# One DMA per store, k and q as one tile, and a new order in a fused attention and MLP kernel

## Chip, cores, metric

The kernel runs on one core of one Trainium2 chip. The time is the device time of one execution in microseconds, and a quoted time is the median of several runs. Each experiment was timed next to the kernel before, in alternating rounds on the same chip. Chips differ a little: the kernel before took 361.2 to 364.1 us on the ones used here. So each experiment is judged by its ratio to the kernel before of its own call. Ratios use fast runs only; where a run was slow (over 1.5% above the fastest of the same kernel), the text says so.

## The reference

Eight batches, eight heads, 576 tokens and 64 channels per head. Attention with random features, then a token mix of rank 32, then a two-layer channel MLP with a residual. All inputs and the output are float32.

```python
def phi(x):                                       # 128 random features: cos and sin
    proj = np.einsum('bhsd,md->bhsm', x, omega)
    return np.concatenate([np.cos(proj), np.sin(proj)], axis=-1) / np.sqrt(m)
q_p, k_p = (phi(q), phi(k))
kv = np.einsum('bhsm,bhsd->bhmd', k_p, v)
z = np.sum(k_p, axis=2)
num = np.einsum('bhsm,bhmd->bhsd', q_p, kv)
den = np.einsum('bhsm,bhm->bhs', q_p, z)          # kept away from zero
x = (num / den)                                   # heads joined: 8 x 576 x 512
# ...
h = x.transpose(0, 2, 1) @ U @ V                  # token mix
u = x + h.transpose(0, 2, 1)
out = u + np.maximum(u @ w_ch1, 0.0) @ w_ch2      # 512 -> 2048 -> 512
```

## The kernel before

Two heads are a group and two groups are a quad. A quad's k, q and v are three loads. k and q of the first four quads are transposed on TensorE; those of the other twelve go through DMA transposes. ScalarE makes the sines and cosines. TensorE then makes `kv` (L416) and `num` (L430), VectorE divides, and a batch's x is complete. The token mix gives u; a DMA transpose on SyncE's queue gives `uT`; then follow the two layers, w1 (L585) and w2 (L605), the residual (L621) and the store (L628).

The program order of all engines is one long string of words. An instruction waits for its operands, but each engine, and each queue that issues DMAs, takes its work in that order.

```python
ORDER = """
begin first/k om ident gate first/q ld/k/0 warm ld/q/0 ldv/0 ld/k/1 cast/k/0 cast/k/1 ...
# ... about 1100 words: load, transpose, layer 1 of batch b, layer 2, store
"""
# ...
rawp = ctx.enter_context(tc.tile_pool(name="rawp", bufs=2))
outp = ctx.enter_context(tc.tile_pool(name="outp", bufs=3))
# ...
held["v", n] = rawp.tile([P, 2, NS * D], F32, name="vraw", bufs=1)       # v of a quad, 576 KB
(nc.sync if n else nc.gpsimd).dma_start(held["v", n], quad(v, n))
# ...
def tpd(name=name, n=n):                                                  # k and q apart
    nc.sync.dma_start_transpose(transposed(name, n), held.pop((name, n)).rearrange("p i e -> p (i e)"))
# ...
def ut0(p=p, cs=cs):                                                      # first token mix, transposed
    t_ps = one(("ut0", p))
    for t in range(NT):
        nc.tensor.matmul(t_ps[:, t * P:(t + 1) * P], held["x", 0][:, t, cs], ident, start=(t == 0), stop=False)
    nc.tensor.matmul(t_ps, held["hu", 0][:, cs], Vb[:, 0:SM], start=False, stop=True)
# ...
add(("tu", b), SP, lambda b=b: nc.sync.dma_start_transpose(
    new_uT(b).rearrange("p t c s -> p (t c) s"), held["u", b].rearrange("p t c -> p (t c)")), ...)
# ...
def store(b=b, t=t, cs=cs, es=(0, 1), by=nc.sync):
    for e in es:
        if b == TAIL:
            dst = out[2 * t + e].rearrange("(p s) c -> p s c", s=NS)[:, 8, cs]
        else:
            dst = out[b].rearrange("(p s) c -> p s c", s=NS)[:, 2 * t + e, cs]
        by.dma_start(dst, held["o", b, t][e * TL:(e + 1) * TL, cs])
```

Token `9*p + 2*t + e` of a batch lies in tile t on partition `64*e + p`, with p from 0 to 63. So one output tile (128 partitions x 512) is two sets of 64 tokens, e = 0 and e = 1. Each set is a regular pattern in memory: 64 rows of 2 KB, nine rows apart. Each store is one DMA per set. The ninth tokens of two batches share the tiles of a "tail" batch.

## Time and profile before

| | before |
|---|---|
| median of 3 runs | 364.13 us |
| span of the profiled run | 359.2 us |
| TensorE (PE) busy | 342.2 us, 95% |
| PE not busy, first 36 us | 36.00 − 25.82 = 10.2 us |
| PE not busy, all the rest | 17.0 − 10.2 = 6.8 us, 4.4 us of it after the last matmul |

From the profile page of the kernel before come the span, busy time of each engine, then rows with one digit per fortieth of the span (9 is 90% or more busy, `PEclk` is the granted TensorE clock in tenths), then the chain of work that ended last by engine, and two kinds of DMA issues with size and median time to landing.

```profile
span 359.2 us, 8233 instructions
PE 342.2 (95%) x3565; PEld 181.2 (50%) x3565; DVE 193.4 (54%) x284; ACT 216.4 (60%) x223; POOL 117.7 (33%) x103
...
PE   4769999999999899999999999999999999999995
...
PEclk9979999999999999999999999999999999999999
DMA  8999899699998895936679705504204145002133
...
PE 85%; DMA 8%; DVE 2%; POOL 2%; issue 1%; ACT 1%; POOLq 0%; DVEq 0%
...
out_dram<-o SPq DMA_DIRECT2D x70, 128.0 KB, 2.9
vraw<-in_v_dram SPq DMA_DIRECT2D x15, 576.0 KB, 4.8
```

TensorE bounds this kernel. After the third slice its row is nearly all nines, and it is 85% of the chain. The DMA engines are also near full for the first third. The loss that remains is in the opening, where the clock row has a 7.

From the wait lists of the kernel before: PE's three longest entries, then one of POOL's (engine, line, what it waited for: total us, times, longest).

```profile
PE ps L317 <- DVE kraw L286: 4.3, 1, 4.3
PE ps L317 <- DMA kraw<-in_k_dram: 3.2, 3, 1.6
PE ps L416 <- POOL vq L301: 1.7, 1, 1.7
...
POOL vq L301 <- DMA vraw<-in_v_dram: 16.7, 5, 6.9
```

All of PE's waits of more than half a microsecond but the 1.7 us are in the opening. Later there are none worth naming: every other transfer is there in time.

From the windows view of the kernel before (stretch, its length, then busy time of PE, PEld, DVE, ACT, POOL with counts, granted clock, DMA share, GB/s):

```profile
core 0: us, PE busy (x) PEld busy (x) DVE busy (x) ACT busy (x) POOL busy (x), PEclk, DMA share, GB/s
0.00:36.00 36.00, 25.82 (x422) 19.32 (x423) 28.18 (x51) 25.63 (x25) 27.14 (x36) 0.91 1.07 203
72.00:108.00 36.00, 35.76 (x480) 19.01 (x479) 26.98 (x38) 26.64 (x25) 15.68 (x14) 1.00 1.19 195
144.00:180.00 36.00, 36.00 (x468) 19.68 (x465) 25.39 (x37) 28.03 (x25) 12.99 (x9) 1.00 0.66 129
252.00:288.00 36.00, 36.00 (x375) 18.64 (x373) 11.05 (x23) 17.86 (x22) 5.51 (x4) 1.00 0.21 52
...
24.00:26.00 2.00, 1.87 (x46) 1.64 (x41) 1.94 (x3) 2.00 (x2) 1.88 (x6) 0.50 1.23 207
```

PE is all but gapless at full clock in the three later stretches, and at half clock from 22 to 28 us.

### The profile page before, as it was taken

Reading aid. Unit: us, or ns where it says so; the run is one execution under the profiler, and the core shown is the slowest. Engines: PE = TensorE matmul, PEld = TensorE weight load, DVE = VectorE, ACT = ScalarE, POOL = GpSimd, SP = SyncE. Lnnn points to the kernel's source line nnn. Section 1 sums busy time; section 2 is a strip of 40 time slices with the busy share of each in tenths; the row PEclk is TensorE's granted clock in tenths of the full one; section 3 lists DMA queues with packets and bytes.
Section 4 is the critical chain, followed back from the end, with each engine's and each line's share of the span. In section 5 each row is a group of like instructions: output and inputs, shape, how many; then the busy total and the mean of one; then the engine's idle time right before and its main releaser. Section 6 shows DMA issues by size and latency. Waiting matters only on the chain.

```text
span 359.2 us, 8233 instructions
## 1 busy us (share of the span) xinstructions
PE 342.2 (95%) x3565; PEld 181.2 (50%) x3565; DVE 193.4 (54%) x284; ACT 216.4 (60%) x223; POOL 117.7 (33%) x103
## 2 busy tenths in 40 slices
PE   4769999999999899999999999999999999999995
PEld 3557455454555464545555454554454544444443
DVE  3989858785888368758645654464132452001111
ACT  4796995749957777696946459536646303651200
POOL 6895670726434724146245124002302100000000
PEclk9979999999999999999999999999999999999999
DMA  8999899699998895936679705504204145002133
GB/s 207 223 234 150 150 190 162 145 187 203 208 186 185 187 215 111 227 53 100 139 195 202 149 2 114 144 2 86 63 2 124 31 93 113 0 2 58 29 70 79
DMA packets 68728, 45.09 MB, mean 126 GB/s; under 512 B 47444, under 2 KB 59860, under 8 KB 68692
## 3 DMA queue, kind: packets, MB, share of 16 engines
q1 hardware_dynamic: 55508, 29.98, 39.8%
q0 software_dynamic: 12816, 13.93, 24.2%
q8 instruction: 28, 0.46, 0.5%
q10 hardware_dynamic: 368, 0.66, 0.5%
q14 instruction: 8, 0.07, 0.1%
HBM read 37.18 MB, written 9.44 MB: 130 GB/s over the span
## 4 chain that ended last, share of the span: by engine, by line
PE 85%; DMA 8%; DVE 2%; POOL 2%; issue 1%; ACT 1%; POOLq 0%; DVEq 0%
PE ps L585 34%; PE ps L605 32%; PE ps L416 5%; PE ps L430 4%; DMA kraw<-in_k_dram 3%; DMA uT<-u 2%; DMA qraw<-in_q_dram 2%; PE ps L392 2%; PE ps L551 2%; PE ps L376 2%; DMA vraw<-in_v_dram 1%; DVE ang L353 1%; PE ps L493 1%; PE ps L435 1%; PE ps L317 1%
## 5 line engine op out<-in xcount | busy, mean ns | idle before, releaser
L402 ACT ACTIVATE ft<-ang 128x2304 bf16<-128x2304 int16 (+3 forms) x70 | 134.7, 1955 | 27.2 <-DVE ang L353 9.7
L598 ACT ACTIVATE hid<-ps 128x512 bf16<-128x512 f32 x144 | 82.5, 597 | 92.7 <-PE ps L585 92.4
L605 PE MATMUL ps<-W2b,hid 128*128 128x512 bf16 (+1 forms) x592 | 134.9, 374 | 0.0
L585 PE MATMUL ps<-uT,W1b 128*128 128x512 bf16 x512 | 119.9, 379 | 0.2 <-DMA uT<-u 0.2
L406 POOL TENSOR_SCALAR ang<-ang 128x2304 int32<-128x2304 int32 (+2 forms) x34 | 67.9, 2000 | 127.7 <-ACT ft L402 113.8
L353 DVE TENSOR_SCALAR ang<-ps 128x1280 int32<-128x1280 f32 (+2 forms) x66 | 85.1, 1317 | 34.7 <-PE ps L369 15.8
L605 PEld LDWEIGHTS <-hid 128*128 128x128 bf16 x592 | 55.5, 98 | 62.8 <-issue 2.3
L585 PEld LDWEIGHTS <-W1b 128*128 128x128 bf16 x576 | 53.9, 98 | 63.8 <-issue 1.4
L621 DVE TENSOR_TENSOR o<-ps,u 128x512 f32<-128x512 f32 x32 | 21.8, 686 | 65.2 <-PE ps L605 64.9
L301 POOL CAST vq<-vraw 128x1152 bf16<-128x1152 f32 x16 | 18.4, 1153 | 30.5 <-DMA vraw<-in_v_dram 16.7
L416 PE MATMUL ps<-vq,ft 64*128 64x65 bf16 x1152 | 25.9, 196 | 2.2 <-POOL vq L301 1.7
L416 PEld LDWEIGHTS <-ft 64*128 64x128 bf16 x1152 | 23.2, 97 | 9.2 <-issue 6.5
L446 DVE TENSOR_TENSOR x<-ps,rec 128x640 bf16<-128x640 f32 x32 | 26.4, 825 | 1.1
L430 PEld LDWEIGHTS <-ft 128*128 128x128 bf16 x512 | 20.2, 99 | 6.4 <-issue 0.8
L430 PE MATMUL ps<-kvb,ft 128*128 128x65 bf16 x512 | 21.6, 195 | 0.0
L420 DVE CAST kvb<-ps 128x260 bf16<-128x260 f32 x32 | 13.1, 423 | 15.3 <-PE ps L416 15.1
L553 DVE TENSOR_TENSOR u<-ps,x 128x1024 bf16<-128x1024 f32 x16 | 19.2, 1219 | 3.6 <-PE ps L551 3.5
L444 DVE RECIPROCAL ps<-ps 128x10 f32<-128x10 f32 x32 | 7.2, 225 | 19.0 <-PE ps L435 19.0
L585 PE MATMUL ps<-utailT,W1b 128*128 128x512 bf16 x64 | 14.6, 379 | 0.0
L392 PE MATMUL ps<-qT,WT 64*128 64x512 bf16 x64 | 14.0, 414 | 0.2 <-DVE ang L353 0.2
L376 PE MATMUL ps<-WT,kT 64*128 64x128 bf16 x256 | 13.8, 233 | 0.3 <-DVE qT L321 0.3
L376 PEld LDWEIGHTS <-kT 64*128 64x128 bf16 x256 | 9.4, 101 | 6.8 <-issue 5.7
(63 smaller groups left out, 152.5 us busy)
## 6 DMA issues: line engine op xcount, KB each, us to landing
out_dram<-o SPq DMA_DIRECT2D x70, 128.0 KB, 2.9
vraw<-in_v_dram SPq DMA_DIRECT2D x15, 576.0 KB, 4.8
kraw<-in_k_dram POOLq DMA_DIRECT2D x15, 288.0 KB, 6.7
qraw<-in_q_dram POOLq DMA_DIRECT2D x15, 288.0 KB, 7.4
W1b<-in_moe_w_ch_dram POOLq DMA_DIRECT2D x4, 512.0 KB, 10.1
W2b<-in_moe_w_ch_dram POOLq DMA_DIRECT2D x4, 512.0 KB, 9.5
vraw<-in_v_dram POOLq DMA_DIRECT2D x1, 576.0 KB, 5.3
ang<-in_k_dram ACTq DMA_DIRECT2D x1, 288.0 KB, 3.2
```

Source lines behind the costliest of these rows:

```text
L353: nc.vector.tensor_scalar(out=dst, in0=src, scalar1=TO_UNITS, scalar2=None, op0=ALU.mult)
L376: nc.tensor.matmul(pk[:, e, j * P:(j + 1) * P], kT[r, c, :], WT[r, :])
L392: nc.tensor.matmul(pq[:, e, :], WT[r, :], held["qT", n][r, c:c + 4, :])
L402: nc.scalar.activation(out=held["ft", g].rearrange("p f a c -> p f (a c)")[:, f, lo:hi], in_=low[:, lo:hi, 0], func=ACT.Sin, scale=TO_RAD)
L406: nc.gpsimd.tensor_scalar(out=ang, in0=ang, scalar1=TURN / 4.0, scalar2=1.0, op0=ALU.add, op1=ALU.mult)
L416: nc.tensor.matmul(kv_ps[:, hh, o], ft[r, f, 0, c:c + M], vq[n % NV][r, NS * (g % 2) + s, :], start=(s == 0), stop=(s == NS - 1))
L430: nc.tensor.matmul(nd[:, hh, t, :], ft[:, f, 1, c:c + P], kvb[:, hh, f, :], start=(f == 0), stop=(f == 1))
L446: nc.vector.tensor_tensor(out=x[:, :, hp * P:(hp + 1) * P].rearrange("p t (h d) -> p h t d", h=2), in0=nd[:, :, :, 0:D], in1=rec.unsqueeze ...
L585: nc.tensor.matmul(one(key), W1b[:, f // 4, ct, f % 4 * P:(f % 4 + 1) * P], uT[:, :, ct, :], start=(ct == 0), stop=(ct == NCT - 1))
L598: nc.scalar.activation(out=held["hid", b][:, f, :], in_=one(at_bank), func=ACT.Relu)
L605: nc.tensor.matmul(one(key)[:, 0:cs.stop - cs.start], held["hid", b][:, f, t * P:(t + 1) * P], W2b[:, f, cs], start=(f == 0), stop=(f == N ...
L621: nc.vector.tensor_tensor(out=held["o", b, t][:, cs], in0=one(key)[:, 0:cs.stop - cs.start], in1=u[:, t, cs], op=ALU.add)
```

## The change

The intent was to fill the opening and to issue fewer DMAs. It has five parts:

1. k and q of a quad share one raw tile and one transposed tile, and one DMA transpose moves both.
2. A store is one DMA of 256 KB, where it was two of 128 KB.
3. The first token mix is split in two: the product with x can start before the low-rank sum is ready, and its last copy is shared by VectorE and ScalarE.
4. Twenty matmuls on the identity matrix (128x512, results unused) stand in PE's order, most of them in the opening, to keep TensorE's clock up.
5. A new order of all the words.

```diff
-begin first/k om ident gate first/q ld/k/0 warm ld/q/0 ldv/0 ld/k/1 cast/k/0 cast/k/1 ld/q/1 omb tpp/k/0/0@2 ...
+begin first/k om ident first/q ld/k/0 d/0@6 warm d/1@2 ld/q/0 d/2@4 ld/k/1 d/3@0 d/4@5 ld/q/1 omb d/5@6 cast/k/0 ...
 (the rest of the order is cut)
+    for i in range(WARMERS):
+        def warmer(i=i):
+            nc.tensor.matmul(one(("d", i)), ident, ident.unsqueeze(1).to_broadcast([P, NT, P]))
 ...
-        if (name, n) not in held:
-            held[name, n] = rawp.tile([P, 2, NS * D], BF16, name=f"{name}raw")
-        return held[name, n]
+        if ("raw", n) not in held:
+            held["raw", n] = rawp.tile([P, 2, 2, NS * D], BF16, name="raw")
+        return held["raw", n][:, "kq".index(name), :, :]
 ...
-                def tpd(name=name, n=n):
-                    nc.sync.dma_start_transpose(transposed(name, n), held.pop((name, n)).rearrange("p i e -> p (i e)"))
-                add(("tp", name, n), SP, tpd, needs=[("ld", name, n)] + old)
+            def tpd(n=n):
+                transposed("k", n)
+                nc.sync.dma_start_transpose(held["T", n].rearrange("p j c s -> p (j c) s"), held.pop(("raw", n)).rearrange("p j i e -> p (j i e)"))
+            add(("tp", n), SP, tpd, needs=[("ld", "k", n), ("ld", "q", n)] + old)
 ...
-        def ut0(p=p, cs=cs):
+        def ut0x(p=p, cs=cs):
             (the four matmuls of x, on their own)
+        add(("ut0x", p), PE, ut0x, needs=[("x", p)], takes=1)
+        add(("ut0", p), PE, lambda p=p, cs=cs: nc.tensor.matmul(one(("ut0x", p)), held["hu", 0][:, cs], Vb[:, 0:SM], start=False, stop=True),
+            needs=[("huc0", p), ("ut0x", p)])
+        pieces = [(0, NT, SCA if p in (1, 2) else DVE)] if p < 3 else [(0, 2, DVE), (2, NT, SCA)]
 ...
-            def store(b=b, t=t, cs=cs, es=(0, 1), by=nc.sync):
-                for e in es:
-                    if b == TAIL:
-                        dst = out[2 * t + e].rearrange("(p s) c -> p s c", s=NS)[:, 8, cs]
-                    else:
-                        dst = out[b].rearrange("(p s) c -> p s c", s=NS)[:, 2 * t + e, cs]
-                    by.dma_start(dst, held["o", b, t][e * TL:(e + 1) * TL, cs])
+            def store(b=b, t=t, cs=cs, es=slice(0, 2), by=nc.sync):
+                if b == TAIL:
+                    dst = out[2 * t + es.start:2 * t + es.stop].rearrange("b (p s) c -> b p s c", s=NS)[:, :, 8, cs]
+                else:
+                    dst = out[b].rearrange("(p s) c -> s p c", s=NS)[2 * t + es.start:2 * t + es.stop, :, cs]
+                by.dma_start(dst, held["o", b, t][es.start * TL:es.stop * TL, cs])
```

## The prediction

> **What bounds it now.** TensorE. The busy table gives PE 342.2 of 359.2 us; the chain that ended last is 85% PE, mostly L585 and L605 at 0.216 us a matmul. In windows from 36 us to the tail PE is idle about 2.5 us, 1.7 of it at 117 us (a late v load, by the waits view). The loss is in the opening: PE is busy 25.8 of the first 36 us, part of it slow. Nine transposes take 1.14 us at 10 and 22 us but 0.68 at 20 us; the granted clock is 0.50 from 22 to 28 us. VectorE is busy 24.8 of 27 us from 9 to 36 us and sets when the first token mix is done (w1 runs freely from 37 us).
>
> **What the change does.**
> 1. Order and split mix: VectorE no longer does group 5's projections (1.49 + 1.22 us) before the last piece of the first mix; group 3's last cosine no longer stands behind a 2.13 us sine; half an eviction (0.35 us) goes to ScalarE. Estimate: first layer 3 to 4 us earlier, 1 us of work deferred: gain 2.5 us.
> 2. Identity matmuls: 20 of 128x512. The Trainium skill, "TensorE: Matmul & The Clock Gate", "What's actually happening", says an idle array drops to half clock; the trace agrees (0.50). They shorten PE links by 0.3 us each, but VectorE is near full: gain 1 us. Those in dense PE work cost 0.216 us each, 0.9 us.
> 3. One transpose for k and q, 18 blocks instead of two of 9: same packets, fewer issues (1.3 to 3.7 us of SyncE each). No PE time; it waits for both loads.
> 4. One DMA per store. The sides are now 2x64x512 in memory and 128 partitions in SBUF. The Trainium skill, "DMA: Bandwidth & Descriptors", "Why a DMA increments its semaphore by 16 and not by 1", says the number of engines divides the slowest dimension of both sides: 16 before (64 rows), 2 after. The trace supports it: the load of V, slowest dimension 4, ran with 4.2 packets in flight at 14 to 17 us, other v loads with 10 to 16. [...]a 256 KB store needs 64 x 0.08 = 5.2 us on two engines, against 2.9 us from issue to landing now. The 32 stores put 167 us on two engines that carry a DMA share of 0.6 to 1.2 until 200 us. SyncE's transposes and v loads queue behind them. The tail batch's stores merge to 128 rows and stay wide.
>
> **Critical path.** Three stores stand directly before batch 5's transpose of u: 15.6 us of queue, then 4 us, against some 10 us of PE work ahead of w1/5: 9 us of PE wait. Around batch 3's transpose and quad 11's another 3 to 8 us. Waits 10 to 20 us, minus 3 to 5 us gained: **374 us**, range **361 to 386**. Faster by over 2%: 0.07; within 2%: 0.33; slower by over 2%: 0.60.
>
> **What shows it.** Right: stores landing in 5 us and more, a store's packets two at a time; PE waits on uT<-u or T<-raw of several us between 90 and 240 us; PE nearly gapless before 36 us, no clock of 0.50; w1 free at 33 us. Wrong: stores still near 3 us, PE idle after 36 us below 3 us.
>
> **What would make it wrong.** If stores still use 16 engines: about 359.5 us. If slack absorbs the queue: about 362. If the two engines saturate from 90 to 240 us: over 385.

## The result and the profile after

| | before | after |
|---|---|---|
| median | 364.11 us (4 runs, 363.94 to 364.51) | 417.63 us (4 runs, 415.88 to 418.64) |
| span of the profiled run | 359.2 us | 416.9 us |
| PE busy | 342.2 us | 360.7 us |
| PE not busy, first 36 us | 10.2 us | 36.00 − 29.50 = 6.5 us |
| PE not busy, all the rest | 6.8 us | 56.2 − 6.5 = 49.7 us |

The ratio is 1.1463, with a 95% interval from 1.1422 to 1.1504. Here and below a ratio is the mean time of one kernel's fast runs over that of the other's of the same rounds, so it is not quite the ratio of the medians quoted.

The profile page after, same parts as before (the landing time of SyncE's DMAs is empty where the page could not pair an issue with its landing):

```profile
span 416.9 us, 8197 instructions
PE 360.7 (87%) x3585; PEld 187.0 (45%) x3585; DVE 194.4 (47%) x284; ACT 217.2 (52%) x224; POOL 117.8 (28%) x103
...
PE   8599899927999995199979997299999499799996
...
PEclk9689999975999996689989999779999779999999
DMA  8999999599959826999759402970312103821022
...
PE 61%; DMA 28%; DVE 4%; ACT 1%; POOL 1%; SPq 1%; issue 1%; POOLq 1%; DVEq 0%; ACTq 0%
...
out_dram<-o SPq DMA_DIRECT2D x35, 256.0 KB
vraw<-in_v_dram SPq DMA_DIRECT2D x15, 576.0 KB
```

PE's row has holes now: a 2 in slice 9, a 1 in slice 17, a 2 in slice 26. The clock row falls just behind each hole. DMA's share of the chain went from 8% to 28%.

The wait lists after, of PE (top three), DVE and POOL:

```profile
PE ps L593 <- DMA uT<-u: 16.6, 2, 8.8
PE ps L420 <- POOL vq L304: 13.8, 2, 9.6
PE ps L396 <- DVE ang L357: 4.6, 2, 4.3
...
DVE o L629 <- DMA out_dram<-o: 20.2, 8, 4.5
...
POOL vq L304 <- DMA vraw<-in_v_dram: 55.3, 9, 15.8
```

L593, L420 and L304 are L585, L416 and L301 of before. PE now waits for `uT`, and for v (which POOL widens first, so PE's wait names POOL, and POOL's wait names the load). VectorE waits for stores, because it needs a free output buffer.

The windows after:

```profile
core 0: us, PE busy (x) PEld busy (x) DVE busy (x) ACT busy (x) POOL busy (x), PEclk, DMA share, GB/s
0.00:36.00 36.00, 29.50 (x446) 19.34 (x447) 27.01 (x50) 25.20 (x26) 26.95 (x37) 0.86 1.03 203
72.00:108.00 36.00, 26.36 (x342) 15.23 (x341) 18.30 (x28) 19.57 (x19) 12.31 (x12) 0.81 0.94 133
144.00:180.00 36.00, 22.90 (x194) 10.93 (x192) 14.02 (x18) 12.31 (x9) 12.07 (x8) 0.77 0.72 100
252.00:288.00 36.00, 26.00 (x178) 11.71 (x173) 11.18 (x17) 5.19 (x7) 1.20 (x2) 0.86 0.52 62
...
20.00:22.00 2.00, 2.00 (x55) 1.80 (x54) 1.18 (x2) 2.00 (x2) 1.96 (x5) 0.50 1.22 214
```

The first 36 us have 3.7 us more PE work than before, of which the identity matmuls are a part. From 72 us on PE is idle for 9.6 to 13.1 us in each of these stretches. GB/s falls from 195 to 133 and from 129 to 100: the DMA engines move less, although there is as much to move.

Two pieces of the chain of work that ended last, after (start, us, what):

```profile
75.25 19.52 DMA vraw<-in_v_dram
...
94.91 1.14 POOL vq L304
...
96.09 1.18 PE ps L420 x36
...
157.93 18.40 DMA uT<-u
...
176.37 4.65 PE ps L593 x11
```

A load of v takes 19.5 us where 4.8 us was the median, and a transpose of u takes 18.4 us. The trace also records every packet of a transfer, and there one can watch both. A load of v has 256 packets of 2304 bytes, a store 128 of 2048.

The v load that was issued at 75.25 us: 224 packets had ended by 83.46 us, with up to 16 in flight. The next packet started at 91.37 us, and the last 32 then ran two at a time until 94.38 us. The two stores issued just before it, from 73.91 us on, ended at 91.35 us. They ran two packets at a time until 83 us and then one at a time, beside packets of a load of k or q; from 89 to 91 us no more than 2.7 packets of any kind were in flight, so most engines had nothing to do. So 32 of 256 packets, which is the share of two engines of sixteen, stood behind the stores. The same 32 packets of each v load ended 0.2 to 1.6 us after the other 224 in 11 of the last 14 loads after, and 10.9, 3.6 and 6.2 us after them in the other three. Before, 1.5 us was the most.

The transpose of u that was issued at 157.93 us, counted from the packet records in windows of one microsecond (number started; mean in flight):

```
us         transposes: started, in flight    stores: started, in flight
166-167    402, 8.3                          13, 1.2
167-168     68, 17.2                         11, 1.1
168-169      0, 18.0                         11, 1.0
169-170      0, 18.0                         23, 2.0
170-174      0, 18.0 in each                 25, 2.1 in each
174-175    850, 20.3                          0, 0.1
175-176    728, 13.3                          4, 0.3
```

The transpose started, stood still with 18 packets in flight, and went on in the microsecond in which the stores ended. PE waited for it 8.8 us, until 176.4 us. It happened again at batch 5: 468 packets from 260 to 263 us, then hardly one until the stores ended at 268 us, then 1574 in two microseconds, and PE waited 7.8 us.

SyncE's timeline shows the same stall at the issuing side. A transpose that is let through is issued in a few microseconds (4.5 us at most in the kernel before). Batch 3's transpose of u before; then those of batches 3 and 5 after (start, us to issue):

```profile
144.06 1.84 SPq L566 DMA_TRANSPOSE uT<-u  x1
...
157.93 16.38 SPq L574 DMA_TRANSPOSE uT<-u  x1
255.25 12.97 SPq L574 DMA_TRANSPOSE uT<-u  x1
```

In the kernel after eight transposes took more than 7 us to issue, and each of them came right after a store in SyncE's order; of the others none took more than 5.6 us. The three late loads of v also came right after a store, and the other eleven did not. Only one transfer that came right after a store was not late: it was issued at 346.7 us, when that store had ended (at 333 us). So what is late is what SyncE issues next after a narrow store that still runs.

### The profile page after: what moved, and what is told of

It reads as the page before. It is cut to its first block, busy times and chain, and to the rows that moved or that the text cites. A ratio compares the mean times of both kernels' runs of the same rounds, so it can differ in the third digit from the quotient of the medians.

```text
span 416.9 us, 8197 instructions
## 1 busy us (share of the span) xinstructions
PE 360.7 (87%) x3585; PEld 187.0 (45%) x3585; DVE 194.4 (47%) x284; ACT 217.2 (52%) x224; POOL 117.8 (28%) x103
## 4 chain that ended last, share of the span: by engine, by line
PE 61%; DMA 28%; DVE 4%; ACT 1%; POOL 1%; SPq 1%; issue 1%; POOLq 1%; DVEq 0%; ACTq 0%
PE ps L593 24%; PE ps L613 22%; DMA uT<-u 8%; DMA vraw<-in_v_dram 8%; DMA out_dram<-o 7%; PE ps L434 4%; PE ps L420 4%; DMA W1b<-in_moe_w_ch_dram 3%; DMA raw<-in_q_dram 3%; PE ps L380 1%; PE ps L559 1%; ACT ft L406 1%; PE ps L396 1%; PE ps L228 1%; DVE o L629 1%
## 5 line engine op out<-in xcount | busy, mean ns | idle before, releaser
L406 ACT ACTIVATE ft<-ang 128x2304 bf16<-128x2304 int16 (+2 forms) x70 | 135.5, 1958 | 42.1 <-POOL ang L410 26.5
L593 PE MATMUL ps<-uT,W1b 128*128 128x512 bf16 x512 | 125.6, 392 | 20.4 <-DMA uT<-u 16.6
L613 PE MATMUL ps<-W2b,hid 128*128 128x512 bf16 (+1 forms) x592 | 139.6, 381 | 2.3 <-DVE o L629 2.3
L593 PEld LDWEIGHTS <-W1b 128*128 128x128 bf16 x576 | 55.8, 100 | 88.3 <-issue 18.8
L420 PE MATMUL ps<-vq,ft 64*128 64x65 bf16 x1152 | 27.9, 204 | 16.4 <-POOL vq L304 13.8
L304 POOL CAST vq<-vraw 128x1152 bf16<-128x1152 f32 x16 | 18.3, 1145 | 74.4 <-DMA vraw<-in_v_dram 55.3
L420 PEld LDWEIGHTS <-ft 64*128 64x128 bf16 x1152 | 24.7, 102 | 24.1 <-issue 18.2
L424 DVE CAST kvb<-ps 128x260 bf16<-128x260 f32 x32 | 13.3, 424 | 34.7 <-PE ps L420 30.1
L434 PE MATMUL ps<-kvb,ft 128*128 128x65 bf16 x512 | 23.1, 201 | 0.0
L396 PE MATMUL ps<-T,WT 64*128 64x512 bf16 x64 | 13.8, 402 | 5.4 <-DVE ang L357 4.6
L380 PE MATMUL ps<-WT,T 64*128 64x128 bf16 x256 | 13.5, 225 | 4.2 <-DVE ang L357 1.9
L551 DVE CAST hu<-ps 128x512 bf16<-128x512 f32 x7 | 4.8, 689 | 22.4 <-PE ps L497 20.9
L593 PE MATMUL ps<-utailT,W1b 128*128 128x512 bf16 x64 | 14.8, 379 | 0.0
```

What stands on the lines that cost most here:

```text
L304: nc.gpsimd.tensor_copy(vq[n % NV][:, :, 0:D], held.pop(("v", n)).rearrange("p i (s d) -> p (i s) d", d=D))
L406: nc.scalar.activation(out=held["ft", g].rearrange("p f a c -> p f (a c)")[:, f, lo:hi], in_=low[:, lo:hi, 0], func=ACT.Sin, scale=TO_RAD)
L420: nc.tensor.matmul(kv_ps[:, hh, o], ft[r, f, 0, c:c + M], vq[n % NV][r, NS * (g % 2) + s, :], start=(s == 0), stop=(s == NS - 1))
L434: nc.tensor.matmul(nd[:, hh, t, :], ft[:, f, 1, c:c + P], kvb[:, hh, f, :], start=(f == 0), stop=(f == 1))
L593: nc.tensor.matmul(one(key), W1b[:, f // 4, ct, f % 4 * P:(f % 4 + 1) * P], uT[:, :, ct, :], start=(ct == 0), stop=(ct == NCT - 1))
L613: nc.tensor.matmul(one(key)[:, 0:cs.stop - cs.start], held["hid", b][:, f, t * P:(t + 1) * P], W2b[:, f, cs], start=(f == 0), stop=(f == N ...
```

## The experiments

The first reading was that the stores of part 2 cost all of it and the other parts almost nothing. That left four ways in which narrow stores could cost so much more than predicted:

- **Queue**: SyncE issues transposes and loads in order, and they stand behind stores that take long to issue. This was the prediction's mechanism, as it was priced.
- **Engines**: the two engines that carry the stores are full, and whatever else needs them waits, whoever issued it.
- **Buffers**: stores end late, so VectorE waits for output buffers.
- **Clock**: each wait cools TensorE down, and what follows runs at half clock.

### Which part is it

**a_two** is the kernel after with two DMAs per store again.

```diff
-                by.dma_start(dst, held["o", b, t][es.start * TL:es.stop * TL, cs])
+                for e in range(es.start, es.stop):
+                    (dst of set e, as in the kernel before)
+                    by.dma_start(dst, held["o", b, t][e * TL:(e + 1) * TL, cs])
```

> The changed kernel with each store in two DMAs of 64 partitions again, all else kept. Theory (stores confined to two DMA engines hold up the transposes and v loads behind them): nearly all of the 53 us goes, 357 to 362 us, stores land in about 3 us, PE waits after 36 us below 12 us, no clock of 0.50 after 36 us. Rival (the merged k and q transpose, whose issue took a median of 4.8 us, or the new order): still over 390 us, waits on uT and v of many us stay.

Measured: 360.62 us against 361.20 us, ratio 0.9972 (0.9907 to 1.0037). In its trace PE is idle for 8.2 us after 36 us, where it was 49.7 us, and no half clock is left there.

**b_one** is the kernel before with only the store of the kernel after (the last part of the diff above, nothing else).

> The kernel before with one DMA per store, nothing else changed. Theory: 385 to 425 us, a store's packets two in flight at a time and 5 to 8 us per store, PE waits on uT or on v of several us each and half clock after them. Rival (transposes or order to blame): within 2% of 364 us.

Measured: 419.23 us against 361.20 us, ratio 1.1578 (1.1501 to 1.1654).

The two runs bracket it: undoing the store takes all of the loss away, and the store alone brings all of it. PE's waits in b_one stand partly at other places, because its order is the old one, but they are of the same kind (wait list of PE in b_one, top two):

```profile
PE ps L416 <- POOL vq L301: 18.3, 3, 7.5
PE ps L369 <- DMA qT<-qraw: 11.7, 3, 6.0
```

**a_two_cold** is a_two without the 20 identity matmuls.

```diff
-begin first/k om ident first/q ld/k/0 d/0@6 warm d/1@2 ld/q/0 d/2@4 ...
+begin first/k om ident first/q ld/k/0 warm ld/q/0 ...      (all d/ words gone)
```

> The changed kernel with stores in two DMAs and all 20 identity matmuls taken out. If they are worth what I predicted (1 us gained in the opening, 0.9 us paid in dense work), 0 to 2 us slower or faster than with them: 358 to 363 us. If the clock in the opening matters more, 3 us and more slower. Half clock lasts until about 18 us and returns once before 30 us.

Measured: 358.76 us, ratio 0.9922 (0.9853 to 0.9992). With them it was 0.9972; the intervals overlap, so no effect of the identity matmuls is shown.

**a_two_oldorder** is a_two without identity matmuls and in the order of the kernel before. The merged transpose stands where the later of the two stood, and one load of k moved behind transpose 10, because the shared tile is free only then.

```diff
-(the order of the kernel after)
+(the order of the kernel before; tp/n at the later of tp/k/n and tp/q/n; ld/k/12 behind tp/10)
```

> Stores in two DMAs, merged k and q transposes, first mix in two parts, but the order of the kernel before (two words moved where the merged transpose forces it) and no identity matmuls. Theory: the merged transpose and the split mix are worth little by themselves: 362 to 365 us, within 0.5% of before. If the merged transpose itself hurts, over 367 us.

Measured: 373.86 us, ratio 1.0322 (1.0267 to 1.0376). This is a miss by some 10 us. Parts 1 and 3 in the old order are not free. Which of them it is, b_mix and a_two_split tell below.

### How narrow stores cost time

**a_act** issues the narrow stores from ScalarE's queue. SyncE then has only transposes and loads, so no store stands in front of them in its queue.

```diff
-            def store(b=b, t=t, cs=cs, es=slice(0, 2), by=nc.sync):
+            def store(b=b, t=t, cs=cs, es=slice(0, 2), by=nc.scalar):
```

> The changed kernel with its narrow stores (2x64x512) issued from ScalarE's queue instead of SyncE's. They still run on two engines, two packets in flight, 5 to 6 us per store. Theory (the transposes and v loads stood behind the stores in SyncE's queue): at least half of the 53 us comes back, 362 to 388 us. Rival (the two engines lack the bandwidth, whoever stands in which queue): still over 400 us. ScalarE itself may lose some by waiting for outputs.

Measured: 417.61 us against 361.58 us, ratio 1.1533 (1.1457 to 1.1609). The top of PE's wait list in a_act, two of its next lines and the one for v; then one line of SyncE's timeline:

```profile
PE ps L593 <- DMA uT<-u: 16.8, 4, 8.9
PE ps L396 <- issue: 5.3, 1, 5.3
PE ps L420 <- ACT hid L606: 4.2, 1, 4.2
...
PE ps L420 <- POOL vq L304: 0.4, 1, 0.4
...
264.74 12.79 SPq L337 DMA_TRANSPOSE T<-raw  x1
```

The total did not move, but the waits did. PE still waits 16.8 us for `uT`, against 16.6 us, now at four places. Its wait for v fell from 13.8 to 0.4 us, and the last 32 packets of a v load ended at most 4.0 us after the others, where it had been 10.9 us. In its place PE waits for ScalarE: that engine's store at 253.4 us took 6.2 us to issue, and the 4.2 us wait for `hid` ended right after it. So the order in SyncE's queue did decide how late v was, and a_act traded that wait for others.

What falls is the queue as the whole explanation. With no store in SyncE's queue a transpose of k and q still took 12.8 us to issue (7.7 us at most in a_wide below, whose stores are not narrow). The Trainium skill says of issuing engines ("DMA: Bandwidth & Descriptors", "Issuing engines are not separate DMA queues") that whichever engine starts a DMA, it runs on the same 16 DMA engines. For the total this run agrees: the ratio is 1.1533 with ScalarE issuing and 1.1463 with SyncE, with medians of 417.61 and 417.63 us. How much the queue alone costs is not shown, because ScalarE has work of its own behind the stores; an issuer with nothing else to do was not tried.

**a_out5** gives the output five buffers where it had three.

```diff
-    outp = ctx.enter_context(tc.tile_pool(name="outp", bufs=3))
+    outp = ctx.enter_context(tc.tile_pool(name="outp", bufs=5))
-            need = [("w2", b, t, 3)] + ([("st", (i - 3) // NT, (i - 3) % NT)] if i >= 3 else [])
+            need = [("w2", b, t, 3)] + ([("st", (i - 5) // NT, (i - 5) % NT)] if i >= 5 else [])
```

> The changed kernel with five output buffers instead of three, narrow stores kept. If VectorE's 20 us of waits for stores to free an output buffer carry the loss: under 395 us. Theory (queueing of transposes and v loads carries it): 405 to 418 us, those waits gone or nearly so and the waits on uT and v still there.

Measured: 409.77 us, ratio 1.1316 (1.1240 to 1.1391). VectorE's waits for stores are gone from its list. PE's two longest entries are still there:

```profile
PE ps L593 <- DMA uT<-u: 18.9, 2, 10.4
PE ps L420 <- POOL vq L304: 13.2, 2, 9.0
```

Buffers are a small part of it, and not the main cause: 1.1463 − 1.1316 is 0.015 of 362 us, some 5 us, and against a_act it is 417.61 − 409.77, some 8 us.

**a_wide** keeps one DMA per store but lays tokens out as (p, e) on the partitions, where they were (e, p). The memory side is then 64 x 2 x 512, so its slowest dimension is 64. The layouts of q's features, U and V follow.

```diff
-            units(held["ang", g][:, 1, P:HALF].rearrange("m (t e p) -> m e t p", e=2, p=TL),
+            units(held["ang", g][:, 1, P:HALF].rearrange("m (t p e) -> m e t p", e=2, p=TL),
 (U loaded per tile, V cast to the same layout)
-                    dst = out[b].rearrange("(p s) c -> s p c", s=NS)[2 * t + es.start:2 * t + es.stop, :, cs]
+                    dst = out[b].rearrange("(p s) c -> p s c", s=NS)[:, 2 * t:2 * t + 2, cs]
```

> The changed kernel, still one DMA per store, but with the two tokens of a position on neighbouring partitions, so that the store is 64x2x512 with 64 as its slowest dimension. Theory (the number of engines is what hurts): within 1% of the version with two DMAs per store, 356 to 363 us, over ten packets of a store in flight, stores landing in about 3 us. Rival (one 256 KB DMA where there were two of 128 KB is what hurts): over 390 us.

Measured: 356.88 us, ratio 0.9853 (0.9778 to 0.9928). So one DMA per store is not what costs: one DMA of the same bytes with another slowest dimension is no slower than two. The late-landing shares of v loads are also gone: 1.8 us is the most in this run.

**a_wide_cold** is a_wide without the identity matmuls (the same edit as in a_two_cold).

> Stores in one wide DMA (64x2x512) and no identity matmuls: if the identity matmuls cost what the pair of runs with two DMAs showed (0.5%), 1 to 3 us faster than the wide version with them and the fastest so far: 355 to 360 us.

Measured: 358.38 us, ratio 0.9904 (0.9830 to 0.9978). Against 0.9853 the sign is the other way round than between a_two and a_two_cold, and again the intervals overlap. Whether the identity matmuls help stays open; they do neither much good nor much harm.

### Where narrow stores cost time

**a_late** has narrow stores in batches 6 and 7 only (8 of 32), where almost nothing else is loaded.

```diff
+                if 6 <= b < TAIL:
+                    dst = out[b].rearrange("(p s) c -> s p c", s=NS)[2 * t:2 * t + 2, :, cs]
+                    by.dma_start(dst, held["o", b, t][:, cs])
+                    return
+                (else two DMAs, as in a_two)
```

> Stores in two DMAs, except for batches 6 and 7 (8 of the 32), whose stores are one narrow DMA each, when nearly all loads and transposes are over. If each narrow store costs its even share of the loss (57 us over 32, 1.8 us each): 372 to 376 us. If they harm only through the loads and transposes beside them: 357 to 364 us.

Measured: 360.35 us against 361.83 us, ratio 0.9950 (0.9892 to 1.0008). No cost of these 8 stores is seen: a_two has 0.9972.

**a_early** has them in batches 0 to 2 only (12 of 32), next to loads and transposes.

```diff
-                if 6 <= b < TAIL:
+                if b < 3:
```

> Stores in two DMAs, except for batches 0, 1 and 2 (12 of the 32), one narrow DMA each, while loads and transposes run all the time. Even share: 380 to 383 us. If they harm through the loads and transposes beside them: 380 to 395 us, with waits on v, uT or T of several us between 80 and 190 us and half clock after them.

Measured: 390.75 us, ratio 1.0782 (1.0724 to 1.0840); one of four runs was slow (395.70 us) and is left out of the ratio. Against a_two that is 1.0782 − 0.9972 = 0.081 of 362 us, or 29 us for 12 stores, some 2.4 us each. A store of the same shape costs nothing that these runs resolve late and 2.4 us early. What it costs is set by what stands beside it. The places are those of the kernel after (top two of PE's wait list in a_early):

```profile
PE ps L420 <- POOL vq L304: 10.0, 1, 10.0
PE ps L593 <- DMA uT<-u: 8.9, 1, 8.9
```

**a_fill** tests the clock. The trace of the kernel after has 55.3 us at half clock from 36 us to its end, that of before none. PE was busy in 30.1 of these 55.3 us. (The 57 us in the expectation below counts some 2 us after the end.) a_fill puts 124 more identity matmuls in front of the five longest waits, so that TensorE stays busy in them.

```diff
+ 36 d/ words ahead of kv/10/0, 14 ahead of aq/20, 32 ahead of w1/3/0, 28 ahead of w1/5/0, 14 ahead of kv/30/0
```

> The changed kernel, narrow stores kept, with 124 more identity matmuls placed in front of the five longest PE waits (36, 14, 32, 28 and 14 of them, 0.216 us each, a little less than the waits). If the half clock that follows a wait costs the 13 us that I work out from the trace, 5 to 12 us faster than the changed kernel, 405 to 412 us, with half clock after 36 us down from 57 us of time to under 25. If the half clock costs nothing beyond the waits: 416 us or more.

Measured: fast runs 409.40, 412.54 and 415.47 us against 361.83 us, ratio 1.1390 (1.1295 to 1.1486). The profiled run was a slow one (416.62 us); in its trace 17.9 us are at half clock after 36 us, where 55.3 us were. So two thirds of the half clock went, and the time fell by little: 1.1463 − 1.1390 is 0.007 of 362 us, some 3 us, and the medians of the fast runs differ by 417.63 − 412.54, some 5 us. The two intervals overlap, so not even this gain is clear of the noise. The expected gain was 5 to 12 us. A possible reading is that the half clock is mostly hidden, because the work that it slows is followed by another wait for a transfer, which absorbs it; but the filling matmuls may also have held up some work, so this is a reading and not a proof.

**a_two_split** is a_two with k and q apart again, in the new order.

```diff
-            add(("tp", n), SP, tpd, needs=[("ld", "k", n), ("ld", "q", n)] + old)
+                add(("tp", name, n), SP, tpd, needs=[("ld", name, n)] + old)
 (and two raw and two transposed tiles; tp/n becomes tp/k/n tp/q/n in the order)
```

> Stores in two DMAs and k and q in tiles of their own again, each with its own transpose, the two issued one after the other where the merged one stood; all else as the changed kernel. If the merged transpose is worth little: within 1% of the version with it, 357 to 363 us. If the merged tile was what made the old order 12 us slower, it should be faster here, under 357 us.

Measured: two fast runs, 358.85 and 361.15 us, and two slow ones, 366.61 and 365.54 us. Ratio of the fast ones 0.9941 (0.9865 to 1.0018). In the new order no difference is shown between one tile for k and q and two.

### How many engines are enough

The number of engines can be set by the number of rows. The Trainium skill ("DMA: Bandwidth & Descriptors", "Why a DMA increments its semaphore by 16 and not by 1") gives the rule: the largest number up to 16 that divides the slowest dimension of both sides. 57 rows give three.

**a_k3** cuts each set of 64 rows into 57 and 7, so most of a store runs on three engines, with 40 packets for each (19 and 1 of each set).

```diff
+                    for lo, hi in ((0, 57), (57, TL)) if b < TAIL else ((0, TL),):
+                        by.dma_start(dst[lo:hi], held["o", b, t][e * TL + lo:e * TL + hi, cs])
```

> The changed kernel with each store in four DMAs, 57 and 7 rows of each half: 57 has no divisor up to 16 but 3 and 1, so the larger ones should run on 3 engines, 40 packets of a store on each, 3.2 us at 0.08 us each instead of 5.2. If harm is in proportion to the time for which a store holds its engines: 390 to 397 us. If it starts only when the few engines have more work than time: 360 to 375 us.

Measured: fast runs 384.00, 384.87 and 381.66 us against 362.53 us, ratio 1.0575 (1.0504 to 1.0645). In the trace (a slow run, 390.85 us) stores run with 3.0 to 3.7 packets in flight from 236 to 242 us, where little else moves, which agrees with the skill's rule.

**a_k16x4** is its control: 48 and 16 rows, so four DMAs per store, all wide.

```diff
-                    for lo, hi in ((0, 57), (57, TL)) if b < TAIL else ((0, TL),):
+                    for lo, hi in ((0, 48), (48, TL)) if b < TAIL else ((0, TL),):
```

> Control of the run on 3 engines: the same four DMAs per store, but of 48 and 16 rows of each half, which divide by 16. Only the issue time of SyncE grows: within 1% of two DMAs per store, 357 to 364 us.

Measured: 362.62 us, ratio 0.9992 (0.9928 to 1.0057). Four DMAs per store cost nothing against two, so it is the engines that cost in a_k3, not the number of DMAs.

**a_k3half** cuts only the second set, so the busiest engines have 24 packets (19 and 1 of the second set, 4 of the first).

```diff
-                    for lo, hi in ((0, 57), (57, TL)) if b < TAIL else ((0, TL),):
+                    for lo, hi in ((0, 57), (57, TL)) if b < TAIL and e else ((0, TL),):
```

> The changed kernel with the first half of each store on 16 engines and the second in DMAs of 57 and 7 rows, so about 20 packets of a store on each of 3 engines. In proportion to the 22 us for 40 packets: 10 us over two wide DMAs, 370 to 374 us. If small loads fit between the other traffic (loss grows faster than the load): 360 to 366 us.

Measured: fast runs 365.27, 361.89 and 365.69 us against 363.58 us (one slow, 369.56 us), ratio 1.0016 (0.9933 to 1.0100).

Together with the others this is a curve:

| packets of a store on its busiest engine | kernel | ratio |
|---|---|---|
| 8 | a_two, a_k16x4, a_wide | 0.997, 0.999, 0.985 |
| 24 | a_k3half | 1.002 |
| 40 | a_k3 | 1.058 |
| 64 | after, b_one | 1.146, 1.158 |

At 24 packets no loss is resolved (the interval reaches 1.0100); from there to 64 it grows by about 1.3 us per packet ((1.146 − 1.002) x 364 us / 40). A straight line from 8 to 64 packets would give about 1.04 at 24, which is outside that interval. A cost that starts only above a certain load is what a full resource gives, and not what a fixed cost per packet gives. The number of engines changes with the packets here, so the two are not separated.

### What was left over

**b_mix** is the kernel before with only the split first mix (part 3).

```diff
 (in the order: ut0/0@2 becomes ut0x/0@2 ut0/0, and so on)
-        def ut0(p=p, cs=cs):
+        def ut0x(p=p, cs=cs):       (and ut0, as in the change)
```

> The kernel before with only the first token mix in two parts (and its last eviction split): within 1% of before, 358 to 363 us. Then, by elimination, the merged k and q tile made the old order 12 us slower. If this run is over 368 us, the split mix did it.

Measured: 364.22 us against 362.53 us, ratio 1.0038 (0.9977 to 1.0100). The split mix is free in the old order. So of the parts in a_two_oldorder only the merged tile is left to cost 12 us there, while no cost of it is seen in the new order (a_two_split). That is by elimination: no run has the merged tile alone in the old order.

**a_wide5** repeats a_wide with five rounds.

> The wide version again, five rounds: the first three gave a ratio of 0.985. 0.980 to 0.992 here, 355 to 359 us, faster than both kernels.

Measured: 358.12 us against 362.53 us, ratio 0.9862 (0.9815 to 0.9910); one of six runs was slow (365.83 us).

**b_wide** is the kernel before with only the wide single store.

```diff
 (the kernel before, with the layout and the store of a_wide)
```

> The kernel before with one wide DMA per store (64x2x512) and nothing else. If wide single stores alone make the best version: 355 to 359 us, a ratio near 0.986. If they are worth nothing: 360 to 364 us, and the rest of the gain belongs to the new order and what goes with it.

Measured: 358.66 us against 363.58 us, ratio 0.9866 (0.9790 to 0.9943). The page of b_wide has its stores as:

```profile
out_dram<-o SPq DMA_DIRECT2D x35, 256.0 KB, 3.0
```

A 256 KB store on all engines lands in 3.0 us, as long as a 128 KB store took before. This one part has all of the gain of a_wide. So the best version is the wide single store, alone or with the rest, 1.3 to 1.5% below the kernel before: the intervals of a_wide, a_wide5 and b_wide all lie below 1, and none of the three shows a gain of 2%. It is the intent of part 2, with the other dimension outside.

## Why the prediction was right and wrong

| the prediction | what the runs showed |
|---|---|
| a narrow store runs on two engines, two packets at a time | right: 2.1 in flight |
| 5.2 us per store | right alone: 5.1 to 5.2 us where nothing else moves, partly by luck. The pace of 0.08 us is that of a packet that runs alone (0.081 us in before, 0.084 us in the narrow stores after), but the late stores of before, which it was said to come from, have 4 packets per engine in 0.74 us. Beside loads it was 8 us (two stores from 75.5 to 91.4 us) |
| the tail batch's stores stay wide | right: its packets run with up to 11.0 in flight (404 to 405 us) |
| 9 us of PE wait at batch 5's transpose of u, behind three stores | right: 7.8 us, behind three stores that ran from 252.6 to 268.0 us |
| another 3 to 8 us around batch 3 and quad 11 | 8.8 us at batch 3's transpose alone and 4.3 us before it |
| first layer 3 to 4 us earlier, free at 33 us | nearly right: its first matmul is at 31.5 us, where it was 34.5 us, and a dense row begins at 34.2 us |
| the other parts gain 3 to 5 us | mostly not there: a_two is 0.6 us below before, inside its interval |
| PE nearly gapless before 36 us, no clock of 0.50 | wrong: 6.5 us idle, and 0.50 from 13.4 to 23.7 us |
| **waits 10 to 20 us in all** | **wrong: PE idle after 36 us rose from 6.8 to 49.7 us** |

**The step that failed** is the term "Waits 10 to 20 us". The two profiled runs differ by 416.9 − 359.2 = 57.7 us. PE idle after 36 us is 49.7 − 6.8 = 42.9 us of that. PE busy after 36 us is another (360.7 − 29.5) − (342.2 − 25.8) = 14.8 us, which fits the same matmuls at half clock: half of the 30.1 us for which PE was busy at half clock is 15.1 us. The opening is level: its time is fixed here by the window, and 3.7 us of idle became 3.7 us of work. The mechanism, transfers that stand behind narrow stores, was right; three things made the term too small.

1. *It priced only `uT` and the keys and queries.* The longest wait of all is for v: 9.6 us at 86 us (`kv` of group 10), and 4.2 us more at 326 us (group 30). The prediction says that v loads "queue behind" stores, but has no wait for v in its sum. In the packet records of the three late loads, 7/8 has landed in a few microseconds; the last eighth stands behind stores on two engines.
2. *It counted three places where there were many.* It looked at batch 5, batch 3 and quad 11. After the change eight transposes and three v loads came right after a store that still ran, and all eleven were late. The prediction let a transpose pay for the stores before it once, as a wait for `uT`; in the traces its issue stands as well, for up to 16.4 us, and SyncE issues nothing else in that time. Taking the stores out of that queue didn't help in total (a_act, 417.61 against 417.63 us), so the order in one queue is only a part of it: the two engines also hold up what another engine issues.
3. *It left out what follows from a wait.* Stores that end late hold output buffers (5 to 8 us, a_out5). Late transfers hold tiles that the next transfers need (loads of v wait 19.5 us for v to be widened out of their tile, where it was 5.5 us). Half clock follows the long waits (55.3 us of time after 36 us), though in a_fill, where most of it was gone, only 3 to 5 us came back.

The prediction had the better alternative in its last paragraph: "If the two engines saturate from 90 to 240 us: over 385." The runs fit it: the dose curve is flat up to 24 packets per engine and then rises, and 12 early stores cost 29 us where no cost of 8 late ones is seen. The prediction even named the 167 us of stores and the DMA share of 0.6 to 1.2 on the same two engines, but it did not add the two up. The trace of before has 17 stores' packets between 90 and 240 us. At 5.2 us each they would keep two engines busy for 88 of these 150 us, a share of 0.59. Its windows have a mean DMA share of 0.73 there, of which the same stores, spread over 16 engines, are 0.10. If the rest is spread evenly, each of the two engines has 0.63 + 0.59 = 1.22. This sum is an estimate. Packets overlap, so a share above 1 is possible: the windows of before have 1.26 from 81 to 90 us and 1.40 from 99 to 108 us. But 1.22 for 150 us on end leaves little slack. It does not show that the engines were full all the time. In the trace after only 11 stores' packets ran from 90 to 240 us, and some store packet was in flight for 67 of these 150 us, so they were full in bursts.

**On the identity matmuls**: the Trainium skill ("TensorE: Matmul & The Clock Gate", "What's actually happening") has the clock released after a busy window of about 3.4 us. The trace agrees that a few matmuls now and then are not enough. From 14 to 16 us PE was busy 0.87 of 2 us, and the clock stayed at 0.50 until PE had been busy without a gap from 19.3 us on; it was 1.00 from 23.7 us on. Of the twenty identity matmuls thirteen ran before 9 us and only one (at 18.3 us) in the stretch at half clock.

**What stays open.** Why the issue of a transpose, and with it the whole transpose, stands still while two engines carry stores is seen and not explained. How much of the loss is the order in SyncE's queue, and how much the time of the two engines, is not separated: a_act changed both the queue and what ScalarE has to do. That the merged tile costs 12 us in the old order is shown by elimination only. Whether the identity matmuls gain or lose a microsecond is below what these runs resolve. How the 43 us divide between v, transposes and buffers was not separated further, because they feed each other.

## What to carry to other kernels

When two DMAs are merged into one, look at the slowest dimension of both sides of the result. With one DMA per store (and the token layout that it needs) and nothing else changed, this kernel was 16% slower with 2 outside and 1.3% faster with 64 outside. Price a narrow transfer by the engines that it fills and by what else has a share on them at that time: a wide load ends with its slowest engine, so what is issued right behind a queue on two engines waits for it. Issuing the narrow stores from ScalarE moved these waits and gained nothing in total. Before calling such a cost small, look at everything that is issued behind the narrow transfers, and add the new work to the busy share that those engines already have.

## What the Trainium skill lacked or had wrong

- "DMA: Bandwidth & Descriptors", "Rules for kernel authors": the row on two transfers to disjoint partition halves says to use one 128-partition transfer. For these stores that held only where the memory side had a wide slowest dimension too. Merged with 2 outside the ratio was 1.158 (b_one), with 64 outside 0.987 (b_wide). The row on using all 16 engines has the condition, but the two are not joined.
- The same page has the rule for the number of engines, and it held in every case looked at: 2 (2.1 packets in flight) and 3 for 57 rows (3.0 to 3.7). It does not say what a narrow DMA does to others: a 16-engine load of 256 packets had 224 done and the last 32 waiting 7.9 us for the narrow stores to end. No cost of such a store was seen in quiet stretches, and about 2.4 us in busy ones.
- The same page, on the DMA transpose: a transpose next to ordinary DMAs "needs nothing". For correctness no run here contradicts it. For time it does need something: packets of a transpose stood still for up to 7.4 us while narrow stores ran (before, the longest took 1.4 us), and its issue took up to 16.4 us (before, 4.5 us). No page has this.
- "TensorE: Matmul & The Clock Gate", "What's actually happening": agrees with the clock of 0.50 before and after. No page says how little a cold clock costs when transfers bound the kernel: with some 37 of 55 us of half clock gone (a_fill, by the trace of a slow run), 3 to 5 us came back, which is not clear of the noise.
